# Layer 1 of group 7 as seven block products, with one tail group worked a period earlier, in a fused attention and MLP kernel

## The chip, the cores and the metric

The kernel runs on one core of a Trainium2 chip. The metric is the device time of one execution in microseconds (us). The core's engines run side by side, each with its own queue in program order: PE (TensorE, the matmuls, with its weight loads listed apart as PEld), DVE (VectorE), ACT (ScalarE), POOL (GpSimd) and SP (SyncE, which here only issues transfers). They meet through semaphores. PSUM, the matmuls' output memory, holds 8 banks in this kernel's pools and is full.

## What is computed

Sliding-window attention over 8 batches of 8 heads, 576 positions and 64 channels, and then, over each position's 512 channels, a normalisation and a two-layer MLP with a residual:

```python
scores = q @ k^T / 8                    # per batch and head
mask   = (rel >= 0) & (rel < 64)        # rel = query position - key position
x      = softmax(where(mask, scores, -1e9)) @ v       # heads side by side: 512 channels
xn     = (x - mean) / sqrt(var + 1e-6) * g_ln
out    = x + relu(xn @ w_ch1) @ w_ch2   # w_ch1 is 512 x 2048, w_ch2 2048 x 512
```

## The kernel before, in words

The positions are worked in nine groups of 512. Groups 0 to 7 are the first 512 positions of each batch. Group 8 collects the last 64 positions of all batches; it is built from four "tail groups" of two batches each, numbered 0 to 3. Each group's rows are four blocks of 128 (`kb`).

The loop over `g` (line 950) is called a period here. Period g does the MLP of group g on PE, and threads into it the attention of batch g+1, loads for later batches, and the parts of tail groups. The MLP is a list of `units`; after unit i the functions put into slot i by `at(i, ...)` are issued. So the order on every engine is written out by hand: units and slots say it, and nothing is reordered later. From the trace, periods 5 to 8 begin with PE's first layer-1 matmul at 181.39, 212.20, 240.53 and 266.98 us.

**Attention of a block**: `s_pe` (L319) puts scores into PSUM, `s_exp` (L355) takes the exponential on ACT, `s_mask` (L367) multiplies with the mask on DVE, `b_pe` (L380) multiplies with v on PE, `b_rows` (L402) divides by the sum and takes mean and variance on DVE, `z_step` (L436) normalises on POOL into `z`, and `zt_step` (L471) transposes z into `zT` by a transfer that SP issues. For a batch `part_vB` (L202) also makes a shifted copy of v by two transfers. For a tail group `load_tail` (L97) issues six transfers on SP, `cast_tail` (L111) makes a memset and three casts on POOL, and `t_tail` (L291) transposes, for tail groups 2 and 3 by transfers. `TAILS` (L949) says which tail group is worked in which period: 0 in period 3, 1 in period 5, and 2 and 3 in period 7. In periods 3 and 5 the tail takes part in the branch at line 1116; for period 7 the loop at line 1162 issues both.

**Layer 1** of periods 3 to 7 is `l1` (L501), 16 units: four matmuls of 512 columns into one of two PSUM buffers with the tag "mm", then a relu on ACT into `hrT`. All four blocks of `zT` are read by each matmul.

**Layer 2** is `stage` (L599), seven block products (Strassen's scheme in Winograd's form): the 2x2 blocks of hrT and of w2 are combined by sums on DVE (`s_sums`, L541, and `w2_sums`), and `product(n, p)` (L556) runs eight matmuls of 256 columns, in the order n = 4, 1, 2, 6, 5, 7, 3. The accumulators are pA and pB (tag "mm") and pC (tag "t1"). `post` (L589) and `post_both` (L583) add an accumulator to the residual on DVE, and `store` (L538) sends the rows out.

**Period 8** (group 8) also does layer 1 by seven block products. The sums of w1 are made by `w1_sums` (L805, four tensors of 128x2048 elements), those of zT by `z_sums` (L817). For each of four blocks d of the hidden dimension `l1_product(n, d)` (L675) runs four matmuls of 256 columns. There are three accumulators per d: A takes products 1, 6, 7 and 4 in turn, B product 2, C products 5 and 3. Between them partial sums are taken out. These are the parts:

- `l1_a1(d)`: product 1 to A, copied by ACT to s1; product 2 to B; DVE adds B + s1, POOL takes the relu.
- `l1_a2(d)`: product 5 to C, copied by ACT to s5. `l1_a` is a1 and a2.
- `l1_b(d)`: product 6 onto A, copied by ACT to u2; product 3 onto C; DVE adds C + u2 and takes the relu.
- `l1_c(d)`: product 7 onto A; DVE adds A + s5 and takes the relu.
- `l1_e(d)`: product 4 onto A; ACT takes the relu (L746).

After the first block the order is a(d), c(d-1), b(d), e(d-1). Accumulator A lies in the two "sc" buffers (those of the scores) for d = 0, 1 and 3 and in an "mm" buffer for d = 2; B in "t0"; C in "xps" and "t1" in turn. The plan of period 8 is a generator that is begun at the end of period 7 (`begin_last`, L944). It sets its s_sums and the layer-2 stages in the order 1, 2, 6, 5, 7, 4, 3, the first two parts of product 1 between the last layer-1 products.

Of the kernel before, what the change touches and what calls it, by code (L numbers as in the profile page):

```python
# [18 lines left out]
def kernel(  # L19
# [10 lines left out]
    nc = tc.nc  # L30
# [464 lines left out]
    def mlp_units(g, split=0, three=False, seven=True):  # L495
        hrT = p_hrt.tile([128, NHC, 512], FP16, tag="hrT", name=f"hrT_{g}")
        hv = hrT[:, :, :].rearrange("p (c e) t -> p c e t", e=2)
        sS = {}
        units = []

        def l1(hc):  # L501
            hps = ps_mm.tile([128, 512], FP32, tag="mm", name=f"hps_{g}_{hc}")
# [53 lines left out]
        def product(n, p):  # L556
            which, a, wv = {
                1: ("A", hv[:, :, 0, 0:256], w2v[:, :, 0, 0, :]),
                2: ("B", hv[:, :, 1, 0:256], w2v[:, :, 1, 0, :]),
                6: ("A", sS[2], wT[2]),  # L560
                5: ("C", sS[1], w2v[:, :, 0, 1, :]),
                7: ("A", sS[3], wT[3]),
                4: ("B", hv[:, :, 1, 256:512], wT[4]),
                3: ("C", sS[4], w2v[:, :, 1, 1, :]),
            }[n]
            first = n in (1, 2, 5, 4)
            if p == 0 and n in (1, 2 if last else 4, 5):
                if which == "C" and last:
                    for r in range(2):
                        bank[("C", r)] = ps_t.tile([128, 256], FP32, tag=f"t{r}", name=f"pC{r}_{g}")  # L570
                elif which == "C":
                    bank[which] = ps_t.tile([128, 2, 256], FP32, tag="t1", name=f"p{which}_{g}")
                else:
                    bank[which] = ps_mm.tile([128, 2, 256], FP32, tag="mm", name=f"p{which}_{g}")
            split_c = last and which == "C"
            o = bank[(which, p)][:, :] if split_c else bank[which][:, p, :]
            for c in range(NHC // 2):
                nc.tensor.matmul(  # L578
                    out=o, lhsT=a[:, c, 128 * p:128 * p + 128], rhs=wv[:, c, :],
                    start=(first and (p == 0 or split_c) and c == 0), stop=(c == NHC // 2 - 1), skip_group_check=True,  # L580
                )
# [93 lines left out]
        def l1_product(n, d):  # L675
            w1v = w1g[:, :, :].rearrange("p (a k) (i e m) -> p a k i e m", a=2, e=2, m=128)
            t1, t2, t3, t4 = (zS["sum"][:, m] for m in range(4))
            z = zT[g]
            which, a, b = {
                1: ("A", w1v[:, 0, :, :, 0, :], z[:, 0:2, 0:256]),  # L680
                2: ("B", w1v[:, 1, :, :, 0, :], z[:, 2:4, 0:256]),
                5: ("C", w1S[1], t1),
                6: ("A", w1S[2], t2),
                3: ("C", w1S[4], z[:, 2:4, 256:512]),
                7: ("A", w1S[3], t3),
                4: ("A", w1v[:, 1, :, :, 1, :], t4),
            }[n]
            if n == 1:
                pool, tag = (ps_mm, "mm") if d == 2 else (ps_s, "sc")
                lbank[("A", d)] = pool.tile([128, 2, 256], FP32, tag=tag, name=f"lA_{d}")  # L690
            elif n == 2:
                lbank[("B", d)] = ps_t.tile([128, 2, 256], FP32, tag="t0", name=f"lB_{d}")
            elif n == 5:
                if d % 2:
                    lbank[("C", d)] = ps_t.tile([128, 2, 256], FP32, tag="t1", name=f"lC_{d}")
                else:
                    lbank[("C", d)] = ps_x.tile([128, 4, 256], FP32, tag="xps", name=f"lC_{d}")[:, 0:2]
            o = lbank[(which, d)]
            for r in range(2):
                for kc in range(2):  # L700
                    nc.tensor.matmul(  # L701
                        out=o[:, r, :], lhsT=a[:, kc, 2 * d + r, :], rhs=b[:, kc, :],
                        start=(n in (1, 2, 5) and r == 0 and kc == 0), stop=(kc == 1), skip_group_check=True,
                    )
# [43 lines left out]
        if last:  # L748
# [53 lines left out]

    w1S = {}

    def w1_sums(*which):  # L805
        wv = w1g[:, :, :].rearrange("p (a k) (i e m) -> p a k i e m", a=2, e=2, m=128)
        a11, a12, a21, a22 = (wv[:, b, :, :, a, :] for a, b in ((0, 0), (0, 1), (1, 0), (1, 1)))
        for n in which:
            w1S[n] = p_in.tile([128, NKC // 2, NHC // 2, 128], FP16, tag=f"qk32_{n % 2}", name=f"w1S{n}")
            o = w1S[n][:, :, :, :]  # L810
            x, y, op = {1: (a21, a22, ALU.add), 2: (w1S.get(1), a11, ALU.subtract),
                        3: (a11, a21, ALU.subtract), 4: (a12, w1S.get(2), ALU.subtract)}[n]
            nc.vector.tensor_tensor(out=o, in0=x, in1=y, op=op)

    zS = {}

# [129 lines left out]
        rest, _ = mlp_units(NGRP - 1)  # L946

    rest = None
    TAILS = {3: [0], 5: [1], 7: [2, 3]}  # L949
    for g in range(NGRP):  # L950
        if g == NGRP - 1:
            for _ in rest:
# [5 lines left out]
        def at(i, f, *a):  # L958
            slots[min(i, len(slots) - 1)].append((f, a))
# [156 lines left out]
        elif g > 1 and b < B:  # L1116
# [4 lines left out]
            at(2, s_pe, b, 2)  # L1121
            at(2, s_exp, b, 2, 0, 1)
            at(3, s_mask, b, 2)
            if tail:
                r, i = NGRP - 1, tail[0]
# [24 lines left out]
                at(7, z_step, b, 1)  # L1150
            if g + 2 < B:
                at(5, alloc_qkT, g + 2)
                at(5, after_mask, *((NGRP - 1, tail[0]) if tail else (b, 3)))
# [5 lines left out]
                at(i, z_step, b, j)  # L1159
            for j in range(4):  # L1160
                at((2, 14, 18, {3: 25, 5: 25}.get(b, 23))[j], zt_step, b, j)
        for n, i in enumerate(TAILS.get(g, ()) if b >= B else ()):
            ts = (13, 13, 17, 22) if n else (1, 2, 5, 11)
            at(ts[0], s_mm, NGRP - 1, i)
            at(ts[1], s_mask, NGRP - 1, i)
            at(ts[2], b_step, NGRP - 1, i)
            at(ts[2], z_step, NGRP - 1, i)
            at(ts[3], zt_step, NGRP - 1, i)
        n = g + 2
        if g > 1 and n < B:  # L1170
            if g > 2:
# [22 lines left out]
        for n, i in enumerate(TAILS.get(g + 1, ())):  # L1194
            if n == 0:
                at(15 if g == 2 else 4, load_tail, i)
                at(24 if i < 2 else 18, cast_tail, i)
                at(27 if i < 2 else 22, t_tail, i, 0)
                at(29 if i < 2 else 22, t_tail, i, 1)
            else:  # L1200
                at(25, load_tail, i)
        if len(TAILS.get(g, ())) == 2:
            at(3, cast_tail, TAILS[g][1])
            at(7, t_tail, TAILS[g][1], 0)
            at(7, t_tail, TAILS[g][1], 1)
# [44 lines left out]
```

## Time and profile before

| what | us |
|---|---|
| median of 3 runs (299.96 to 300.1) | 300.01 |
| the profiled execution | 300.26 |
| its span, first to last instruction | 298.5 |
| outside the span | 1.76 |
| mean granted TensorE clock | 0.996 |

The profile is of one execution. Its page gives the busy time of each engine, the chain of work that ended last (followed back from the last instruction to what released it) and the costliest groups of instructions. The trace behind it answers with timelines: start, duration, engine, line, operation, output<-input, shape, count, and in brackets the idle time before and what ended it. Starts are counted from the span's start. A PE row's duration is longer than its share of the engine, because matmuls overlap: the share is the distance to the next row's start. Layer 1 of group 7 runs from 240.53 to 256.01 us on PE, layer 2 from there to 270.11 with the first products of group 8 between.

### The profile page before, as it was taken

The page shows a single profiled execution, that of the slowest core. Times are in us where ns is not written, and L with a number is a line of the kernel's source. Part 1 is how long each engine was busy: PE and PEld are TensorE (multiplying, and loading weights), DVE is VectorE, ACT ScalarE, POOL GpSimd, SP SyncE. Part 2 cuts the span into 40 slices and gives each one's busy share as a digit, 9 for nine tenths or more (in the row PEclk, how much of TensorE's full clock was granted, in tenths as well). Part 3 has the DMA queues.
Part 4 walks back from the last instruction along what each step waited for, and adds up shares of the span by engine and source line. Part 5 has one row for each costly group of instructions (what it writes and reads, how often), then busy time and mean ns, then how long its engine had stood idle before and what let it go on. Part 6 is the DMA issues. An engine that isn't in the chain of part 4 may idle for free.

```text
span 298.5 us, 7825 instructions
## 1 busy us (share of the span) xinstructions
PE 290.9 (97%) x3187; PEld 206.8 (69%) x3187; DVE 218.1 (73%) x413; ACT 154.3 (52%) x261; POOL 166.5 (56%) x244
## 2 busy tenths in 40 slices
PE   8989999999999999999999999999999999999994
PEld 3657545788888888557854786469646854788883
DVE  2881358789994794489767865699568785789983
ACT  3566647677449625873276428841674056305500
POOL 4688889763850987289508860897048407024300
PEclk9999999999999999999999999999999999999998
DMA  8999999979979999899299998991729396003014
GB/s 190 261 377 342 367 302 285 237 226 297 196 168 295 250 133 220 278 222 177 49 308 256 194 176 278 279 162 40 221 50 182 71 185 187 20 18 143 1 37 107
DMA packets 113223, 58.11 MB, mean 195 GB/s; under 512 B 82593, under 2 KB 104161, under 8 KB 113186
## 3 DMA queue, kind: packets, MB, share of 16 engines
q1 hardware_dynamic: 112752, 57.21, 79.1%
q8 instruction: 25, 0.41, 0.6%
q10 hardware_dynamic: 434, 0.40, 0.4%
q14 instruction: 12, 0.10, 0.1%
HBM read 38.80 MB, written 9.44 MB: 162 GB/s over the span
## 4 chain that ended last, share of the span: by engine, by line
PE 93%; DVE 4%; POOL 1%; ACT 1%; issue 0%; POOLq 0%
PE hps L504 26%; PE pA L578 14%; PE hph L645 12%; PE pB L578 10%; PE pC L578 9%; PE xps L399 4%; PE sc L352 3%; PE ch L662 3%; PE tp L279 3%; PE lA L701 2%; PE warm L872 2%; PE lC L701 1%; PE ch L516 1%; PE ztp L481 1%; DVE stats L429 1%; DVE xn L423 1%
## 5 line engine op out<-in xcount | busy, mean ns | idle before, releaser
L504 PE MATMUL hps<-zT,w1g 128*128 128x512 f16 x352 | 80.2, 379 | 0.0
L508 ACT ACTIVATE hrT<-hps 128x512 f16<-128x512 f32 x88 | 52.8, 600 | 36.8 <-PE hps L504 33.8
L504 PEld LDWEIGHTS <-w1g 128*128 128x128 f16 x352 | 33.2, 98 | 38.0 <-issue 1.7
L578 PEld LDWEIGHTS <-sS 128*128 128x128 f16 x512 | 49.3, 98 | 5.6
L362 ACT ACTIVATE pt<-sc 128x512 f16<-128x512 f32 x72 | 39.8, 603 | 22.7 <-PE sc L352 22.3
L451 POOL TENSOR_SCALAR rsz<-mvg 128x1 f32<-128x1 f32 x32 | 10.2, 320 | 61.3 <-DVE mvg L432 51.7
L578 PEld LDWEIGHTS <-hrT 128*128 128x128 f16 x384 | 36.7, 98 | 7.0 <-ACT hrT L508 0.8
L372 DVE TENSOR_TENSOR pt<-pt,mask 128x1024 f16<-128x1024 f16 x32 | 23.9, 753 | 19.6 <-ACT pt L362 19.6
L645 PE MATMUL hph<-zT,w1g 128*128 128x256 f16 x320 | 37.9, 273 | 0.0
L157 POOL CAST qk<-qk 128x1024 f16<-128x1024 f32 x29 | 32.4, 1138 | 8.6 <-PE sc L352 6.0
L645 PEld LDWEIGHTS <-w1g 128*128 128x128 f16 x320 | 30.4, 98 | 4.5 <-POOL w1g L233 0.2
L578 PE MATMUL pC<-w2s,sS 128*128 128x256 f16 x256 | 31.2, 273 | 0.0
L578 PE MATMUL pA<-wT,sS 128*128 128x256 f16 x256 | 30.9, 273 | 0.0
L650 ACT ACTIVATE hrT<-hph 128x512 f16<-128x512 f32 x40 | 24.1, 606 | 10.9 <-PE hph L645 10.7
L260 ACT COPY qkT<-tp 128x1024 f16<-128x1024 f16 (+1 forms) x18 | 17.3, 962 | 23.0 <-PE tp L279 21.3
L552 DVE TENSOR_TENSOR sS<-hrT 128x1024 f16<-128x1024 f16 (+2 forms) x41 | 26.8, 654 | 1.8 <-ACT hrT L508 1.7
L423 DVE TENSOR_TENSOR xn<-xps,rcp 128x256 f32<-128x256 f32 (+1 forms) x50 | 25.8, 539 | 1.5 <-DMA out_dram<-xn 0.8
L429 DVE BATCH_NORM_STATS2 stats<-xn 128x6 f32<-128x512 f32 x36 | 25.0, 694 | 1.2
L457 POOL TENSOR_SCALAR z<-xn,rsz 128x512 f16<-128x512 f32 x24 | 22.3, 927 | 2.5
L452 POOL TENSOR_TENSOR rsz<-rsz,mhalf 128x1 f32<-128x1 f32 x32 | 20.9, 652 | 2.7
L185 POOL CAST vA<-v 128x1024 f16<-128x1024 f32 (+1 forms) x18 | 16.9, 957 | 4.5 <-DMA v<-in_v_dram 4.3
L399 PEld LDWEIGHTS <-pt 128*64 128x64 f16 x576 | 11.5, 110 | 9.1 <-issue 4.7
(121 smaller groups left out, 423.9 us busy)
## 6 DMA issues: line engine op xcount, KB each, us to landing
qk<-in_q_dram SPq DMA_DIRECT2D x16, 512.0 KB, 6.1
qk<-in_k_dram SPq DMA_DIRECT2D x16, 512.0 KB, 7.3
out_dram<-xn SPq DMA_DIRECT2D x32, 256.0 KB, 3.8
v<-in_v_dram SPq DMA_DIRECT2D x28, 256.0 KB, 7.5
w2s<-in_moe_w_ch_dram SPq DMA_DIRECT2D x9, 512.0 KB, 8.5
w1s<-in_moe_w_ch_dram SPq DMA_DIRECT2D x4, 512.0 KB, 7.3
tk<-in_k_dram SPq DMA_DIRECT2D x8, 256.0 KB, 4.4
tv<-in_v_dram SPq DMA_DIRECT2D x8, 256.0 KB, 5.1
```

The costliest lines, as they stand in the source:

```text
L157: nc.gpsimd.tensor_copy(out=dst[:, :].rearrange("p (a j) e d -> p a e j d", j=j), in_=t[:, :].rearrange("p (a e j d) -> p a e j d", e=2, j ...
L362: nc.scalar.activation(out=o, in_=i, func=AF.Exp, bias=0.0, scale=scale)
L372: nc.vector.tensor_tensor(out=ptv, in0=ptv, in1=mb, op=ALU.mult)
L399: nc.tensor.matmul(out=tiles[h // n][64 * r:64 * r + 64, h % n, :D + 1], lhsT=pt[:, par, hp, r, :], rhs=rhs, start=True, stop=True)
L423: nc.vector.tensor_tensor(out=xn[:, n * i:n * i + n], in0=xps[:, :, 0:D], in1=rcp_b, op=ALU.mult)
L429: nc.vector.bn_stats(out=stats, in_=xv)
L504: nc.tensor.matmul(out=hps, lhsT=w1g[:, kc, 128 * hc:128 * (hc + 1)], rhs=zT[g][:, kc, :], start=(kc == 0), stop=(kc == NKC - 1),)
L508: nc.scalar.activation(out=hrT[:, hc, :], in_=hps, func=AF.Relu, bias=0.0, scale=1.0)
L552: nc.vector.tensor_tensor(out=o, in0=x, in1=y, op=op)
L578: nc.tensor.matmul(out=o, lhsT=a[:, c, 128 * p:128 * p + 128], rhs=wv[:, c, :], start=(first and (p == 0 or split_c) and c == 0), stop=(c ...
L645: nc.tensor.matmul(out=hps[:, e], lhsT=w1g[:, kc, 128 * hc:128 * (hc + 1)], rhs=zT[g][:, kc, 256 * half:256 * half + 256], start=(kc == 0) ...
L650: nc.scalar.activation(out=hrT[:, 2 * i:2 * i + 2, 256 * half:256 * half + 256], in_=hps, func=AF.Relu, bias=0.0, scale=1.0)
```

## The change

Period 7 (group NGRP-2) and period 8 are now both "mixed". Period 7's units are layer 1 by seven block products and then the stages in the order 1, 2, 6, 5, 7, 4, 3. The sums of w1 are made in periods 5 and 6 instead of 7, zT's sums are now also made for group 7, at the end of period 6. Tail group 2 is worked in period 6, in the same branch as those of periods 3 and 5, and so is loaded, cast and transposed in period 5; tail group 3 stays in period 7 and is loaded, cast and transposed in period 6. In period 7 accumulator A takes "mm" for every d. In period 7 product 4 of layer 2, and with it the stores of rows 2 and 3, come later than before, and the first units of period 8 one slot later.

```diff
+        mixed = g >= NGRP - 2
...
-            if p == 0 and n in (1, 2 if last else 4, 5):
+            if p == 0 and n in (1, 2 if mixed else 4, 5):
...
-                store(2)
-                store(3)
+                if not mixed:
+                    store(2)
+                    store(3)
...
+                elif mixed:
+                    store(2)
+                    store(3)
...
-                pool, tag = (ps_mm, "mm") if d == 2 else (ps_s, "sc")
+                pool, tag = (ps_mm, "mm") if d == 2 or not last else (ps_s, "sc")
...
+        if mixed:
+            def with_sums(f, a, c0, n):
+                f(*a)
+                s_sums(c0, c0 + 4, n)
+
+            units = [lambda: l1_a1(0), lambda: l1_a2(0), lambda: l1_b(0)]
+            for d in range(1, 4):
+                units += [lambda d=d: l1_a(d), lambda d=d: l1_c(d - 1), lambda d=d: l1_b(d), lambda d=d: l1_e(d - 1)]
+            units[10] = lambda: with_sums(l1_e, (1,), 0, 1)
+            units += [
+                lambda: with_sums(stage, (1, 0), 0, 2), lambda: with_sums(l1_c, (3,), 4, 1),
+                lambda: stage(1, 1), lambda: with_sums(l1_e, (3,), 4, 2),
+                lambda: stage(2, 0), lambda: stage(2, 1),
+            ]
+            for n, m in ((6, 3), (5, 4)):
+                for p in range(2):
+                    units.append(lambda n=n, m=m, p=p: with_sums(stage, (n, p), 4 * p, m))
+            for n in (7, 4, 3):
+                for p in range(2):
+                    units.append(lambda n=n, p=p: stage(n, p))
+            return units, s_sums
...
-    TAILS = {3: [0], 5: [1], 7: [2, 3]}
+    TAILS = {3: 0, 5: 1, 6: 2, 7: 3}
...
-        for n, i in enumerate(TAILS.get(g, ()) if b >= B else ()):
-            ts = (13, 13, 17, 22) if n else (1, 2, 5, 11)
-            at(ts[0], s_mm, NGRP - 1, i)
-            at(ts[1], s_mask, NGRP - 1, i)
-            at(ts[2], b_step, NGRP - 1, i)
-            at(ts[2], z_step, NGRP - 1, i)
-            at(ts[3], zt_step, NGRP - 1, i)
+        if g == NGRP - 2:
+            r, i = NGRP - 1, TAILS[g]
+            at(0, s_pe, r, i)
+            at(2, s_exp, r, i, 0)
+            at(3, s_exp, r, i, 1)
+            at(4, s_mask, r, i)
+            at(7, b_pe, r, i, "sc")
+            at(7, b_rows, r, i)
+            at(7, z_step, r, i)
+            at(11, zt_step, r, i)
...
-        if g > 2:
+        if 2 < g < NGRP - 2:
...
+        if g + 1 in TAILS:
+            i = TAILS[g + 1]
+            at(15 if g == 2 else 4, load_tail, i)
+            at((24, 24, 14, 18)[i], cast_tail, i)
+            at((27, 27, 20, 22)[i], t_tail, i, 0)
+            at((29, 29, 20, 22)[i], t_tail, i, 1)
+        if g == NGRP - 4:
+            at(23, w1_sums, 3, (0,))
+            at(25, w1_sums, 3, (1,))
+        if g == NGRP - 3:
+            at(0, w1_sums, 1)
+            at(3, w1_sums, 2)
+            at(25, w1_sums, 4)
+            at(28, z_sums, NGRP - 2, 1, 2)
+            at(29, z_sums, NGRP - 2, 3, 4)
         if g == NGRP - 2:
-            at(0, w1_sums, 1, 2)
-            at(3, w1_sums, 3)
-            at(21, w1_sums, 4)
-            at(27, z_sums, NGRP - 1, 1, 2)
-            at(28, z_sums, NGRP - 1, 3, 4)
-            at(27, begin_last)
-            at(28, lambda: next(rest))
+            at(25, z_sums, NGRP - 1, 1, 2)
+            at(27, z_sums, NGRP - 1, 3, 4)
+            at(28, begin_last)
+            at(29, lambda: next(rest))
```

In the units of the change a(d) is unit 3, 7 and 11 for d = 1, 2 and 3, and the others follow in the order above: c(d-1), b(d), e(d-1).

More of the change, by code (lines that the diff above doesn't have):

```diff
@@ L688, in l1_product @@
             if n == 1:
-                pool, tag = (ps_mm, "mm") if d == 2 else (ps_s, "sc")
-                lbank[("A", d)] = pool.tile([128, 2, 256], FP32, tag=tag, name=f"lA_{d}")
+                pool, tag = (ps_mm, "mm") if d == 2 or not last else (ps_s, "sc")
+                lbank[("A", d)] = pool.tile([128, 2, 256], FP32, tag=tag, name=f"lA_{g}_{d}")
             elif n == 2:
-                lbank[("B", d)] = ps_t.tile([128, 2, 256], FP32, tag="t0", name=f"lB_{d}")
+                lbank[("B", d)] = ps_t.tile([128, 2, 256], FP32, tag="t0", name=f"lB_{g}_{d}")
             elif n == 5:
                 if d % 2:
-                    lbank[("C", d)] = ps_t.tile([128, 2, 256], FP32, tag="t1", name=f"lC_{d}")
+                    lbank[("C", d)] = ps_t.tile([128, 2, 256], FP32, tag="t1", name=f"lC_{g}_{d}")
                 else:
-                    lbank[("C", d)] = ps_x.tile([128, 4, 256], FP32, tag="xps", name=f"lC_{d}")[:, 0:2]
+                    lbank[("C", d)] = ps_x.tile([128, 4, 256], FP32, tag="xps", name=f"lC_{g}_{d}")[:, 0:2]
             o = lbank[(which, d)]
@@ L803, with w1_sums @@
     w1S = {}
-    def w1_sums(*which):
+    def w1_sums(n, ks=(0, 1)):
         wv = w1g[:, :, :].rearrange("p (a k) (i e m) -> p a k i e m", a=2, e=2, m=128)
         a11, a12, a21, a22 = (wv[:, b, :, :, a, :] for a, b in ((0, 0), (0, 1), (1, 0), (1, 1)))
-        for n in which:
+        if n not in w1S:
             w1S[n] = p_in.tile([128, NKC // 2, NHC // 2, 128], FP16, tag=f"qk32_{n % 2}", name=f"w1S{n}")
[L810 to L813, printed above, removed]
+        x, y, op = {1: (a21, a22, ALU.add), 2: (w1S.get(1), a11, ALU.subtract),
+                    3: (a11, a21, ALU.subtract), 4: (a12, w1S.get(2), ALU.subtract)}[n]
+        k = slice(ks[0], ks[-1] + 1)
+        nc.vector.tensor_tensor(out=w1S[n][:, k], in0=x[:, k], in1=y[:, k], op=op)
     zS = {}
@@ L1123 @@
             at(3, s_mask, b, 2)
-            if tail:
-                r, i = NGRP - 1, tail[0]
+            if tail is not None:
+                r, i = NGRP - 1, tail
                 at(2, s_pe, r, i, False, "t")
@@ L1152 @@
                 at(5, alloc_qkT, g + 2)
-                at(5, after_mask, *((NGRP - 1, tail[0]) if tail else (b, 3)))
+                at(5, after_mask, *((NGRP - 1, tail) if tail is not None else (b, 3)))
                 at(5, cast_qk, g + 2, 0)
@@ L1193 @@
                 at((15, 15, 20, 22)[i - 1], s_sums, 6, 8, i)
[L1194 to L1205, printed above, removed]
-        if g == NGRP - 2:
-            at(0, w1_sums, 1, 2)
-            at(3, w1_sums, 3)
-            at(21, w1_sums, 4)
-            at(27, z_sums, NGRP - 1, 1, 2)
-            at(28, z_sums, NGRP - 1, 3, 4)
-            at(27, begin_last)
-            at(28, lambda: next(rest))
+        if g + 1 in TAILS:
[13 more added lines that the diff above has]
+            at(29, z_sums, NGRP - 2, 3, 4)
+        if g == NGRP - 2:
+            at(25, z_sums, NGRP - 1, 1, 2)
+            at(27, z_sums, NGRP - 1, 3, 4)
+            at(28, begin_last)
+            at(29, lambda: next(rest))
         for i, u in enumerate(units):
```

## The prediction

> **What bounds the kernel now.** I read the page first (busy time, then the chain that ended last), then TensorE's timeline over the last three periods, and the other engines' timelines beside it.
>
> ```profile
> PE 290.9 (97%) x3187; PEld 206.8 (69%) x3187; DVE 218.1 (73%) x413; ACT 154.3 (52%) x261; POOL 166.5 (56%) x244
> ...
> PE 93%; DVE 4%; POOL 1%; ACT 1%; issue 0%; POOLq 0%
> ```
>
> PE is busy for 97% of the span and makes 93% of the chain. So a matmul removed is worth its full time, and a wait added in front of one costs its full time. The stage of the change, from the table of stages (period 7, then period 8 to the end):
>
> ```profile
> 240.70:267.14 26.44, 26.44 (x226) 16.58 (x225) 19.13 (x32) 11.30 (x20) 7.89 (x12) 1.00 0.51 110
> 267.14:298.50 31.36, 26.89 (x241) 23.04 (x238) 23.97 (x44) 9.21 (x16) 6.05 (x4) 0.96 0.23 68
> ```
>
> Columns: span, then busy us of PE, PEld, DVE, ACT, POOL, granted clock, DMA. Period 7 has no hole on PE: 26.44 of 26.44 us. Period 8 already does layer 1 by seven products, the form that period 7 is to get, so it prices the new work. Its rows on PE, ACT and the weight loads:
>
> ```profile
> 246.78 7.08 PE L504 MATMUL hps<-zT,w1g 128*128 128x512 f16 x32
> ...
> 272.30 1.04 PE L701 MATMUL lA<-zsums,w1S 128*128 128x256 f16 x8
> 273.17 0.60 PE L701 MATMUL lC<-zT,w1S 128*128 128x256 f16 x4
> ...
> 282.78 0.60 PE L701 MATMUL lA<-zsums,w1g 128*128 128x256 f16 x4
> ```
> ```profile
> 283.41 0.60 ACT L746 ACTIVATE hrT<-lA 128x512 f16<-128x512 f32 x1 [2.14 <-PE lA L701]
> ```
> ```profile
> 284.06 0.99 PEld L578 LDWEIGHTS <-hrT 128*128 128x128 f16 x10 [0.31 <-ACT hrT L746]
> ```
>
> The reader is to see two prices. A 512-column matmul takes 7.01/32 = 0.219 us (to the next row's start, 253.79), a 256-column one 0.109 (8 in 0.87 us, 272.30 to 273.17). And what PE pays when it must wait for the relu behind product 4: four matmuls issued from 282.78 leave PE's issue free at 283.22, ACT starts at 283.41, ends at 284.01, PE goes on at 284.06. That is **0.84 us** from the end of issue.
>
> **Part 1, fewer columns.** Period 7's layer 1 was 64 matmuls of 512 columns. On PE's timeline they take 1.83 + 3.70 + 7.01 + 1.88 = 14.42 us (64 x 0.219 = 14.0, the rest is restarts after scores and attention). It becomes 7 x 4 x 4 = 112 matmuls of 256 columns, 112 x 0.109 = 12.24, and I leave 0.2 for the two interruptions that stay. Term: **-2.0**. Weight loads are no limit: 0.098 us each beside 0.109.
>
> **Part 2, the accumulator banks.** In period 8 the four A accumulators live in three buffers (d 0, 1, 3 in the two "sc", d 2 in "mm"). In period 7 all four take the two "mm" buffers, because the scores of the tail group need "sc". The order of units is a(d), c(d-1), b(d), e(d-1): product 4 of block d-1 (in e) comes right before product 1 of block d+1, which takes the same buffer. So lA of block 2 waits for the relu of block 0, block 3 for that of block 1, the first layer-2 product pA for that of block 2 and pB for that of block 3; the built program has each of these four matmuls wait on ACT at exactly these relus. Nothing of PE stands between, PE runs in order, and everything behind queues. 4 x 0.84 = **+3.4**. Bounds: 4 x 0.6 (the relu alone) = 2.4, and 4 x 1.0 = 4.0 if a copy of ACT stands in front.
>
> **Part 3, product 3 of block 0.** It reuses bank C after ACT's copy (0.59) of product 5. In period 8 half a pC product (0.87 us) lies between; in period 7 only product 6 (0.44). Copy starts 0.63 after product 5's start and ends at 1.22, product 3 would be due at 0.87: **+0.4** (0 to 0.5).
>
> **Part 4, VectorE's queue.** Product 4 of block d-1 adds onto the A bank that VectorE must have read (the sum after product 7). In period 8 that sum is just in time (276.08 to 276.76, PE due at 276.76). In period 7 the rows of the last tail group are put in slot 7, in front of the sum of block 1. The like rows of before:
>
> ```profile
> 258.63 0.20 DVE L419 RECIPROCAL rcp<-xps 128x8 f32<-128x8 f32 x1
> 258.87 0.69 DVE L423 TENSOR_TENSOR xn<-xps,rcp 128x512 f32<-128x512 f32 x1
> 259.59 0.69 DVE L429 BATCH_NORM_STATS2 stats<-xn 128x6 f32<-128x512 f32 x1
> 260.32 0.18 DVE L432 BATCH_NORM_AGGREGATE mvg<-stats 128x2 f32<-128x6 f32 x1
> ```
>
> They are 1.8 us in a queue without gaps. Counting from the period's start with parts 2 and 3 in: attention of the tail ends on PE at 8.6, its rows are done at 10.5, the sum of block 1 at 11.2, and product 4 was due at 9.8. **+1.4** (0.5 if VectorE is ahead by the slack of part 2's waits, 2.2 if the mask of the same tail also runs late). The other new work of period 7 finds room: 12 copies and 4 relus on ACT replace 16 relus (0.60 each); POOL's four relus (1.5 each) end before layer 2 reads them.
>
> **Part 5, one tail group earlier.** On PE it is moved: 0.34 (scores) + 0.38 (attention) leave period 7 and enter period 6. Net 0. But its loads, casts and transposes move into period 5, where POOL and SP are full:
>
> ```profile
> 199.64 1.21 POOL L157 CAST qk<-qk 128x1024 f16<-128x1024 f32 x1
> ...
> 203.47 2.02 POOL L185 CAST vA<-v 128x1024 f16<-128x1024 f32 x2
> ...
> 207.26 0.76 POOL L457 TENSOR_SCALAR z<-xn,rsz 128x512 f16<-128x512 f32 x1
> ```
> ```profile
> 199.59 9.65 SPq L477 DMA_TRANSPOSE zT<-z  x4
> ```
>
> POOL has no gap from 190.05 to 208.02, where z of group 6's last block ends. The tail's memset and three casts go in before the vA casts: 175.87 to 178.51 in period 4 (2.64), 229.44 to 232.60 in period 6 (3.16). So that z ends at 210.7 to 211.2. SP gets 5.0 more us of loads (221.06 to 226.11 in period 6) and two more transposes (1.2 each) ahead of its transpose and is free at about 210.6, no earlier limit. From issue to landing zT takes 2.3 us there; with the tail's transposes in flight 3.2 is also seen. Landed: 213.0 to 214.4. Period 6's first matmul needs all four blocks and was due at 212.1. **+1.3** (0.9 to 2.3; 0 if POOL's z of 2.17 us at 195.25, otherwise 0.76, is short this time and the casts are cheap). vB, issued behind it, lands at 215.5 before the attention that needs it at 216.1.
>
> **Part 6, sums.** The w1 sums (1.22, 1.22, 1.22, 1.47) and four z sums (2.1) go to periods 5 and 6. VectorE idles 1.7 and 2.0 us early in period 6, so the first two are hidden. Late in it the tail's 2.7 us and the 1.47 make VectorE as tight as in period 5, where the post of product 6 ended 0.4 before PE needed it (207.6, 208.03); period 6 has two transposes (0.9) less on PE. **+0.1** (0 to 1). Period 8 starts with z sums earlier: **-0.1**, the wait of 0.18 that it has now.
>
> **Sum**: -2.0 + 3.4 + 0.4 + 1.4 + 1.3 + 0.1 - 0.1 = **+4.5**. The profiled execution took 300.26 (298.5 in the span), so 304.8; it lies 0.25 above the median of the runs, 300.01. Against the median: **304.5**.
>
> **Rivals.** (a) *Part 5 is hidden*, POOL or the landing has slack that I don't see: +3.2, **303.2**; for it speaks that the one z of 2.17 us is 1.4 above its like. Chance 0.25. (b) *VectorE becomes the bound* in both periods 6 and 7: parts 4 and 6 at their upper ends, and landing at its upper end, +4.5 + 0.8 + 0.9 = **306.2**. VectorE would be some 28 us busy of 29 in period 6 (20.2 + 2.7 tail + 3.9 + 0.9 sums). Chance 0.12. (c) *Faster*: the bank waits cost almost nothing, because the relu of one block overlaps matmuls that PE can still run. Then -2.0 and small waits of 0.5, as in period 8 (its 28 products and two halves of pA and of pC take 16.24 us instead of 15.7): **298.5**. It decides where the release costs under 0.4 us instead of 0.84, together with no wait in part 5; the row at 284.06 and the written order speak against it. Chance 0.04. (d) *Same*: the waits just eat the gain, 300 +- 0.6; it needs parts 4 and 5 both at nothing and part 2 at half. Chance 0.03. (e) *The clock drops*: period 7's layer 1 has 5 us of holes in 20, each of 0.4 to 1.4 us. If the gate counted that as idle and halved the clock, 12 us of matmuls would take 24: **316**. The granted clock is 1.00 from 10 to 20 us, where PE is busy 8.68 of 10, with single holes up to 0.85, so I give 0.02. [...] No run here shows such a drop between matmuls.
>
> **How the numbers follow.** The forecast holds 0.54, the rivals 0.25, 0.12, 0.04, 0.03, 0.02. The range, **302.4 to 306.4**, takes in (a), most of (b) and the bounds of parts 2, 4 and 5, and leaves out (c), (d), (e) and the extremes. Faster than before by over 0.2% (0.6 us, about what a measurement can tell from no change): 0.04; within: 0.03; slower: 0.93.
>
> **What the profile after would show.** 112 more L701 matmuls at 0.109 in period 7 and 64 fewer hps. PE holes of about 0.84, released by ACT's relu, before lA of blocks 2 and 3, pA and pB; one of over 1 us released by VectorE's sum of block 1; one of 1 to 2 us before the first hps of period 6, released by the zT transpose. If the four ACT holes are absent, part 2 is wrong and with it the sign. If PE's hole at period 6's start is absent, (a) holds.

## The result and the profile after

| | before | after |
|---|---|---|
| median of the runs, us | 300.06 (6 runs, 299.83 to 300.26) | 310.2 (6 runs, 308.25 to 312.66) |
| the profiled execution, us | 300.26 | 309.08 |
| its span, us | 298.5 | 307.4 |

The ratio is 1.0348, with a 95% interval of 1.0314 to 1.0381. The kernel became slower by 10.1 us; 4.5 had been forecast, with a range up to 306.4. The runs after also spread over 4.4 us, those before over 0.4.

The page of the changed kernel, busy times, the granted clock in 40 slices of 7.7 us, and the chain:

```profile
PE 291.8 (95%) x3235; PEld 212.0 (69%) x3235; DVE 227.3 (74%) x436; ACT 154.2 (50%) x261; POOL 171.1 (56%) x248
...
PEclk9999999999999999999999999999799999999998
```

PE has 48 matmuls more (112 of 256 columns for 64 of 512) and 0.9 us more of busy time in a span 8.9 us longer. So 8.0 of it are holes. One slice, the 29th (215 to 223 us), has a lower clock. The table of stages (periods 6, 7, and 8 to the end):

```profile
216.09:246.92 30.83, 30.83 (x305) 19.63 (x305) 23.08 (x48) 12.38 (x22) 15.79 (x24) 0.94 0.58 127
246.92:275.94 29.02, 24.81 (x243) 20.76 (x241) 24.02 (x48) 10.21 (x18) 7.88 (x8) 1.00 0.12 42
```

Period 7 took 26.45 us before with PE busy throughout; now it takes 29.02 with PE busy for 24.81, that is 4.21 us of holes. Period 6 took 28.33 before and takes 30.83, busy throughout, at a mean clock of 0.94. It also begins later, at 216.09 instead of 212.20. PE's timeline there, and the holes in period 7:

```profile
210.59 1.92 PE L579 MATMUL pC<-w2s,sS 128*128 128x256 f16 x16
216.09 4.45 PE L505 MATMUL hps<-zT,w1g 128*128 128x512 f16 x12 [3.58 <-DMA zT<-z]
```
```profile
253.97 0.60 PE L706 MATMUL lA<-zT,w1g 128*128 128x256 f16 x4 [0.73 <-ACT hrT L751]
...
258.42 0.60 PE L706 MATMUL lA<-zsums,w1g 128*128 128x256 f16 x4 [1.18 <-DVE hrT L721]
259.70 0.60 PE L706 MATMUL lA<-zT,w1g 128*128 128x256 f16 x4 [0.68 <-ACT hrT L751]
...
263.67 1.03 PE L579 MATMUL pA<-w2s,hrT 128*128 128x256 f16 x8 [0.69 <-ACT hrT L751]
...
267.21 1.91 PE L579 MATMUL pB<-w2s,hrT 128*128 128x256 f16 x16 [0.69 <-ACT hrT L751]
```

The bracket is the idle time before a row and what ended it. The last five rows are the forecast's four bank waits and its wait for VectorE. The first fence holds what was not forecast: a hole of 3.58 us where 1 to 2 had been, and behind it twelve matmuls that take 4.45 us where they took 2.78. The windows there (after the busy times come the granted clock and the DMA share):

```profile
217.00:220.00 3.00, 3.00 (x8) 1.06 (x7) 0.00 (x0) 1.19 (x2) 0.00 (x0) 0.50 0.97 308
220.00:222.00 2.00, 2.00 (x53) 1.17 (x52) 0.97 (x3) 1.30 (x3) 0.00 (x0) 0.94 0.55 208
```

Half the clock, from 216.83 to 220.24 us. And SP's timeline ahead of the hole (the issue of transfers, "x2" for two of them):

```profile
194.74 1.50 SPq L106 DMA_DIRECT2D tq<-in_q_dram  x2
196.28 3.63 SPq L109 DMA_DIRECT2D tk<-in_k_dram  x2
199.95 2.29 SPq L109 DMA_DIRECT2D tv<-in_v_dram  x2
202.34 3.76 SPq L268 DMA_TRANSPOSE qkT<-qk  x2
206.20 4.69 SPq L477 DMA_TRANSPOSE zT<-z  x3
211.06 1.19 SPq L297 DMA_TRANSPOSE tqT<-tq  x1
212.35 1.25 SPq L304 DMA_TRANSPOSE tkT<-tk  x1
213.69 1.23 SPq L477 DMA_TRANSPOSE zT<-z  x1
```

The first three rows and the two for tqT and tkT are the tail group's, new in this period. SP is hardly ever free here (one pause of 0.4 us, at 204.4, lies inside the row of qkT), and the last zT is issued at 213.69 although POOL had its z ready at 211.94. POOL is late too, by 3.9 us against the 208.02 of before: the tail's memset and casts stand in front of the casts of vA, and one of them waits for its load.

```profile
203.61 0.17 POOL L118 MEMSET vt<- 128x16 f16 x1
...
205.83 1.04 POOL L121 CAST vt<-tv 128x1024 f16<-128x1024 f32 x1 [0.57 <-DMA tv<-in_v_dram]
206.81 2.67 POOL L185 CAST vA<-v 128x1024 f16<-128x1024 f32 x2
...
211.18 0.76 POOL L457 TENSOR_SCALAR z<-xn,rsz 128x512 f16<-128x512 f32 x1
```

### The profile page after: what moved, and what is told of

Its sections match the earlier page's. It is cut to its first block, busy times and chain, and to the rows that moved or that the text cites. A ratio compares the mean times of both kernels' runs of the same rounds, so it can differ in the third digit from the quotient of the medians.

```text
span 307.4 us, 7978 instructions
## 1 busy us (share of the span) xinstructions
PE 291.8 (95%) x3235; PEld 212.0 (69%) x3235; DVE 227.3 (74%) x436; ACT 154.2 (50%) x261; POOL 171.1 (56%) x248
## 4 chain that ended last, share of the span: by engine, by line
PE 80%; POOL 7%; DMA 3%; SPq 2%; DVE 2%; issue 2%; ACT 2%; POOLq 0%; ACTq 0%
PE hps L505 18%; PE pA L579 12%; PE hph L650 12%; PE pB L579 8%; PE pC L579 8%; PE lA L706 4%; PE sc L352 3%; PE xps L399 3%; PE ch L667 3%; PE tp L279 2%; PE lC L706 2%; DMA qk<-in_k_dram 2%; POOL qk L157 2%; POOL z L457 2%; PE lB L706 1%
## 5 line engine op out<-in xcount | busy, mean ns | idle before, releaser
L505 PE MATMUL hps<-zT,w1g 128*128 128x512 f16 x288 | 67.4, 386 | 3.6 <-DMA zT<-z 3.6
L509 ACT ACTIVATE hrT<-hps 128x512 f16<-128x512 f32 x72 | 43.2, 600 | 25.3 <-PE hps L505 18.6
L505 PEld LDWEIGHTS <-w1g 128*128 128x128 f16 x288 | 27.4, 99 | 35.7 <-DMA zT<-z 3.9
L372 DVE TENSOR_TENSOR pt<-pt,mask 128x1024 f16<-128x1024 f16 x32 | 25.3, 799 | 14.6 <-ACT pt L362 14.6
L650 PEld LDWEIGHTS <-w1g 128*128 128x128 f16 x320 | 30.4, 98 | 4.6 <-POOL w1g L233 0.3
L723 POOL TENSOR_SCALAR hrT<-hrT 128x512 f16<-128x512 f16 x8 | 11.9, 1487 | 31.9 <-DVE hrT L721 29.3
L553 DVE TENSOR_TENSOR sS<-hrT 128x1024 f16<-128x1024 f16 (+2 forms) x39 | 25.9, 664 | 0.3 <-ACT hrT L509 0.3
L457 POOL TENSOR_SCALAR z<-xn,rsz 128x512 f16<-128x512 f32 x24 | 23.0, 959 | 2.5
L419 DVE RECIPROCAL rcp<-xps 128x4 f32<-128x4 f32 (+1 forms) x51 | 7.9, 178 | 18.0 <-PE xps L399 17.9
```

The source lines that it names most:

```text
L372: nc.vector.tensor_tensor(out=ptv, in0=ptv, in1=mb, op=ALU.mult)
L457: nc.gpsimd.tensor_scalar(out=z, in0=xv, scalar1=rs, scalar2=nm, op0=ALU.mult, op1=ALU.add)
L505: nc.tensor.matmul(out=hps, lhsT=w1g[:, kc, 128 * hc:128 * (hc + 1)], rhs=zT[g][:, kc, :], start=(kc == 0), stop=(kc == NKC - 1),)
L509: nc.scalar.activation(out=hrT[:, hc, :], in_=hps, func=AF.Relu, bias=0.0, scale=1.0)
L650: nc.tensor.matmul(out=hps[:, e], lhsT=w1g[:, kc, 128 * hc:128 * (hc + 1)], rhs=zT[g][:, kc, 256 * half:256 * half + 256], start=(kc == 0) ...
```

## The experiments

Two theories stood at the start. **A**: the miss belongs to the moved tail group: SP's queue makes the hole, and the hole costs the clock. **B**: it belongs to layer 1 by seven products and its sums (VectorE late in two periods). "Period 6's start" below is PE's first layer-1 matmul of that period, 212.20 before and 216.09 after.

**1. The tail's move alone.** Layer 1 of group 7 as before, the sums as before:

```diff
-        mixed = g >= NGRP - 2
+        mixed = g >= NGRP - 1
```

> Only the move of tail group 2 is kept; layer 1 of group 7, the sums of w1 and zT and the order of layer 2 are those of before. Theory: the late zT of period 6 (SP's queue, filled with the tail's loads and transposes) and the half clock behind the hole cost about 5.4 us whatever layer 1 of group 7 does. Expected 305.5 us, PE's hole at the start of period 6 at 3.5 us and the first hps of period 6 at a granted clock of 0.5. Rival: the hole comes from the new sums and layer 1, or from both together, and the tail alone is the +1.3 of the prediction: 301.4 us.

Measured 304.4 us (ratio 1.0153, 1.0121 to 1.0184), nearer to the theory's 305.5 than to the rival's 301.4. PE at the start of period 6:

```profile
215.15 4.36 PE L505 MATMUL hps<-zT,w1g 128*128 128x512 f16 x12 [3.18 <-DMA zT<-z]
```

POOL's z ends at 210.66 here, as forecast, but the last zT is issued at 212.70, behind the tail's transposes. So the hole and the clock belong to the tail's move, and the other 5.8 us of the change come with layer 1 and its sums.

**2. The tail's transposes behind the last zT.**

```diff
-            at((27, 27, 20, 22)[i], t_tail, i, 0)
-            at((29, 29, 20, 22)[i], t_tail, i, 1)
+            at((27, 27, 25, 22)[i], t_tail, i, 0)
+            at((29, 29, 25, 22)[i], t_tail, i, 1)
```

> The changed kernel, with the two transposes of tail group 2 issued in slot 25 of period 5 instead of 20, so that SP issues them behind the last zT of group 6. Theory (SP's queue is the bound): the zT is issued at 212.0, where POOL's z ends, lands at 214.3, the hole shrinks from 3.6 to about 2.0 us, and a hole that short leaves the clock at 1.00: 306.8 us. Rival (POOL's z is the bound, SP only follows): the zT is issued no earlier, no change, 310.2. Second rival (the first matmuls are slow for another reason than the hole's length): 1.7 gained, not 3.4, 308.5.

Measured 310.1 us (1.0307, against the same runs of before). PE's timeline of this kernel:

```profile
214.46 2.78 PE L505 MATMUL hps<-zT,w1g 128*128 128x512 f16 x12 [2.09 <-DMA zT<-z]
219.46 0.23 PE L399 MATMUL xps<-vB,pt 128*64 128x65 f16 x1 [2.22 <-DMA vB<-vA]
...
220.04 0.61 PE L352 MATMUL sc<-qkT,qkT 64*128 64x64 f16 x16
...
221.01 1.46 PE L505 MATMUL hps<-zT,w1g 128*128 128x512 f16 x3
```

The last zT is issued at 212.02, right behind POOL's z (212.00), the hole shrinks to 2.09 us, and the twelve matmuls behind it run at the full clock. So the theory's first step holds, and it divides the hole of 3.58 us: 2.09 stay with POOL's late z, 1.5 were SP's queue. The time is still that of the rival, for another reason. The transfers that build vB now stand behind the tail's transposes (SP issues them at 215.92), the attention of batch 7 waits 2.22 us for them, and behind this second hole the clock is halved after all (0.50 from 219.24 to 222.65). Layer 1 goes on at 221.01, only 0.4 us earlier than without the edit, and its next three matmuls take 1.46 us. What stood last in SP's queue paid: zT with the hole of 3.58 us in the change, vB with one of 2.22 here.

**3. The hole filled with matmuls on zeros** (16 of 512 columns at the end of period 5; they write a bank that nothing reads):

> The changed kernel, with 16 dummy matmuls of 512 columns (3.5 us, on constants, into a fresh buffer that nothing reads) at the end of period 5, in PE's hole. Theory (the idle hole makes the clock gate halve the clock): the hole's length stays, but the matmuls after it run at 0.219 us and a granted clock of 1.00: 1.7 us faster than the change, 308.5. Rival (the first hps are slow because transfers crowd their reads, or for another reason): they stay at 0.43 us each, 310.2 or slower.

Measured 308.25 us (1.0274). In this kernel's timeline the same late start is followed by a full clock:

```profile
212.29 3.62 PE L1258 MATMUL hole<-wfill 128*128 128x512 f16 x16
215.74 2.79 PE L505 MATMUL hps<-zT,w1g 128*128 128x512 f16 x12
```

So it was the idle time that took the clock there: the twelve matmuls take 2.79 us behind the filled hole and 4.45 behind the idle one, 1.7 us more. But this execution shows the clock fall elsewhere, in period 7 behind the holes of 1.18 and 0.69 us (PE's rows, then windows of 3.41 us with the granted clock third from the end):

```profile
254.70 0.60 PE L706 MATMUL lC<-zT,w1S 128*128 128x256 f16 x4
256.48 0.60 PE L706 MATMUL lA<-zsums,w1g 128*128 128x256 f16 x4 [1.18 <-DVE hrT L721]
257.77 0.91 PE L706 MATMUL lA<-zT,w1g 128*128 128x256 f16 x4 [0.69 <-ACT hrT L751]
...
258.48 1.06 PE L706 MATMUL lB<-zT,w1g 128*128 128x256 f16 x4
```
```profile
254.49:257.90 3.41, 1.54 (x14) 1.08 (x12) 3.27 (x9) 1.19 (x2) 2.78 (x5) 1.00 0.01 2
257.90:261.31 3.41, 3.41 (x18) 2.35 (x17) 1.52 (x3) 1.17 (x2) 1.16 (x2) 0.50 0.24 43
261.31:264.70 3.39, 2.71 (x25) 2.28 (x24) 2.54 (x5) 1.18 (x2) 0.60 (x1) 1.00 0.00 0
```

Rows that take 0.60 us elsewhere take 0.91 and 1.06, and period 7 takes 30.6 us instead of 29.0.

**4. Period 7's holes filled too**, with two matmuls on zeros in each of the slots 6, 10, 14 and 18, beside those of experiment 3:

> The changed kernel with dummy matmuls of 512 columns on constants in PE's holes: 16 at the end of period 5, and 2 each before lA of blocks 2 and 3, before pA and after product 4 of block 3 (0.44 us each place, within waits of 0.7), into buffers that nothing reads. The waits themselves stay. Theory (the clock gate counts the holes): the granted clock stays 1.00 in periods 6 and 7 in every execution, all matmuls run at full rate, 306.9 us, and the runs lie within 0.5 us of each other instead of 4. Rival (the clock in period 7 falls for the load itself, whatever PE does in the holes): 308.3 as with the first hole alone filled.

Measured 307.43 us (1.0249, 1.0233 to 1.0266), all runs within 1.25 us. Mean clock 0.998 in the profiled execution (0.992 after), 0.997 to 1.0 in the four runs, and period 7 takes 29.0. So the clock stays up with the holes filled, as the theory says; the time lies between its 306.9 and the rival's 308.3, and the spread is more than its 0.5. Do such drops also explain the 4.4 us of spread of the changed kernel, and its median, 1.1 above the profiled execution, which had no drop in period 7? In part. The mean clock is on record for every run: 0.992 and 0.993 in its two fastest runs and 0.986 to 0.988 in the four others, which fits one more drop in those. But two runs with 0.987 and 0.988 took 309.6 and 312.66 us, and in experiment 3 the slowest run, 310.17, had 0.997. The rest of the spread has another cause, which stays open.

**5. The order of a block's products** in period 7: 2, 5, 1, so that two products stand between product 4's relu and the next user of its bank; likewise the last layer-1 products ahead of pA and pB. It was timed in one execution.

```diff
-                units += [lambda d=d: l1_a(d), ...
+                units += [lambda d=d: l1_251(d), ...
...
-                lambda: with_sums(stage, (1, 0), 0, 2), lambda: with_sums(l1_c, (3,), 4, 1),
-                lambda: stage(1, 1), lambda: with_sums(l1_e, (3,), 4, 2),
+                lambda: with_sums(l1_c, (3,), 4, 1), lambda: with_sums(stage, (1, 0), 0, 2),
+                lambda: with_sums(l1_e, (3,), 4, 2), lambda: stage(1, 1),
```

> The changed kernel, with period 7's block order 2, 5, 1 in place of 1, 2, 5 for d = 1 to 3, and product 7 of block 3 put before the first half of layer 2's product 1, product 4 of block 3 before the second half: two products (0.87 us) now lie between each relu's product 4 and the matmul that takes its bank for blocks 2 and 3 and pB, one (0.44) for pA. Theory: three of the four waits of 0.7 vanish and the fourth is 0.3; period 7, from its first layer-1 matmul to that of group 8, takes 26.6 instead of 29.0 us. Rival (the wait is in fact that of VectorE's sums, the bank only comes last): the holes move to the products behind and the period stays within 0.6 of 29.0.

It took 309.12 us (the profiled execution after took 309.08), and period 7 29.3, which is the rival's figure. The bank waits are gone but for 0.25 at pA, and the wait for VectorE in front of product 4 of block 1 grew from 1.18 to 2.08, with half the clock behind it (0.50 from 260.29 to 263.70):

```profile
259.05 0.60 PE L706 MATMUL lA<-zsums,w1g 128*128 128x256 f16 x4 [2.08 <-DVE hrT L721]
```

One wait had hidden part of another. The rival's figure is in part luck: the drop costs 1.7 us (half of 3.41), and without it the period would be 27.6, an estimate, midway between theory and rival.

**6. The same, and the tail's rows behind layer 1** (slot 18 instead of 7):

> The changed kernel with the block order of the earlier order run, and with the tail's rows on VectorE moved from slot 7 to slot 18 of period 7 (behind layer 1), its scores from slot 0 to slot 1, zT's sums for group 8 to slots 27 and 28. Period 6's late start stays. Theory: the hole before product 4 of block 1 (1.18, or 2.08 in the order run) goes, the bank waits too, so period 7 takes 26.5 us instead of 29.0, PE is never idle long enough in it to lose the clock, and the time is 306.3 us (310.2, less 2.5 for the waits, less 1.4 for the clock in most executions). Rival (VectorE is full in layer 1 whatever the order): holes of 1 us or more move to the next sums, and the period stays above 28.

Measured 306.1 us (1.0216, 1.0187 to 1.0245); period 7 takes 26.49, as expected. With both kinds of wait taken away period 7 still only equals the 26.45 of before, with one tail group less in it.

**7. and 8. The tail groups in periods 3, 4, 5 and 7**, so that period 6 has none; number 8 has the edits of experiment 6 as well:

```diff
-    TAILS = {3: 0, 5: 1, 6: 2, 7: 3}
+    TAILS = {3: 0, 4: 1, 5: 2, 7: 3}
```

> The changed kernel with the tail groups 0 to 3 worked in periods 3, 4, 5 and 7 instead of 3, 5, 6 and 7, and tail 2 transposed on PE as 0 and 1 are (0.7 us of PE). Nothing of a tail is loaded, cast or transposed in period 5, so period 6 starts as before. Theory: the 5.4 us of period 6's start go, layer 1 by seven products as written stays a loss: 300.1 + 2.5 (waits less columns) + 0.7 (transposes) + 1.4 (half clock in period 7 in most executions) = 304.7 us. Rival (layer 1 by seven products is a gain once period 6 starts in time): below 300.

> Both: the tail groups in periods 3, 4, 5 and 7, and the block order and the rows' place of the run before. Theory: no hole at period 6, period 7 at 26.0 to 26.5 us with one tail in it, no clock loss: 300.1 - 2.0 (columns) + 0.5 (left-over waits) + 0.7 (transposes on PE) - 0.1 = 299.2 us. Rival (every earlier period loses as much by its new tail as period 6 did): 302 or more.

Measured 309.84 (1.0328) and 306.55 us (1.0208). Both missed; for number 8 the rival's time (302 or more) came. Period 6 takes 28.33 us again, but in number 7 period 4 takes 35.0 instead of 30.8 and period 3 32.3 instead of 30.7 (33.8 and 33.0 in number 8). PE and POOL of number 7 in period 4:

```profile
181.68 0.40 PE L481 MATMUL ztp<-ident,z 128*128 128x128 f16 x4 [2.18 <-POOL z L457]
```
```profile
180.85 0.77 POOL L457 TENSOR_SCALAR z<-xn,rsz 128x512 f16<-128x512 f32 x1 [2.27 <-DMA zT<-z]
```

There are three z buffers, and each is free only when the transfer that transposes it has read it. SP issues these transfers behind the tail's loads; so POOL waits for them (2.27 us in the row above), and PE for POOL (2.18). In each of the three periods in which it was tried (3 and 4 here, 5 in the change), fetching one tail group while working another beside a batch to load cost time. (Before, periods 3 and 5 worked one and periods 2, 4 and 6 fetched.)

**9. Tail group 2 out of period 5**: loaded behind everything else there, cast and transposed in period 6, its rows late in period 6.

> The changed kernel with tail group 2 taken out of period 5: its loads are issued behind everything else of period 5, its casts and transposes come in slots 9 and 10 of period 6, its scores in slot 17 and its rows in slot 23; tail group 3 is loaded and cast a little later in period 6. Layer 1 of period 7 is left as in the change. Theory (the hole at the start of period 6 and the half clock behind it come from the tail's loads and transposes that stand on SP's queue ahead of the last zT): period 6 starts again at 212.2 instead of 216.1, its first twelve matmuls take 2.7 instead of 4.45 us, period 7 stays at 29.0 to 30.6: 310.2 less 5.4 is 304.8. Rival (period 6 has no room for casts, transposes and rows of one tail and the loads of the other; VectorE becomes late behind its seven-product sums): period 6 takes 31 to 32 us instead of 29, and the time is 306.5 to 308.

**10. The same with the edits of experiment 6.**

> The kernel before this one and, in period 7, the two mends that together brought it to 26.5 us (per block the products in the order 2, 5, 1; the tail's rows behind layer 1). Theory (the two losses are separate and add): 306.1 less the 5.4 of period 6's start, 300.7. With both losses gone layer 1 by seven products is worth almost nothing: period 7 takes 26.5 us as it did before the change. Rival (period 6 is too full with a whole tail in it): 302 to 303.5.

**11. The same with four A banks** instead, in the order of the change, and the tail's attention behind layer 1:

```diff
-                pool, tag = (ps_mm, "mm") if d == 2 or not last else (ps_s, "sc")
+                pool, tag = (ps_mm, "mm") if (d == 2 if last else d < 2) else (ps_s, "sc")
```

> Tail group 2 out of period 5 as in the two kernels ahead, the products of a block in the order of the change (1, 2, 5), but the four A accumulators of period 7 in four banks (two mm, then two sc), and the last tail's attention put into slot 20, behind the layer-1 products that need the sc banks. Theory (what is left of period 7's holes, 1.7 us in seven holes of 0.25 to 0.34, is waits on a bank or on the copy of product 1 that stands too close; with four banks and the order 1, 2, 5 they go, and the 2 us of columns come out as time): period 7 takes 24.9 to 25.3 us and the time is 299.2, below the 300.0 before the change. Rival (VectorE is busy for 23 of these 25 us and sets the pace, and the late tail delays the sums of zT that period 8 starts with): period 7 and the start of period 8 give it back, 300.5 to 301.5.

Measured 307.73 (1.0223), 305.5 (1.0178, 1.0153 to 1.0203) and 302.99 us (1.0106, 1.007 to 1.0142). In all three, period 6 starts at 211.8 to 212.6 with the twelve matmuls in 2.78 us, so that part of theory A held. But period 6 takes 31.75 us, which in number 9 is the rival. Numbers 10 and 11 missed both of their figures; in number 10 period 7 takes 27.99 instead of 26.5, with new waits of 0.77 and 0.41 us near its start. The rows of number 11:

```profile
230.95 0.41 PE L352 MATMUL sc<-tqT,tkT 64*128 64x64 f16 x16 [1.12 <-DMA tkT<-tk]
...
237.06 0.45 PE L399 MATMUL xps<-vt,pt 128*64 128x65 f16 x16 [1.23 <-DVE pt L372]
...
246.50 0.60 PE L706 MATMUL lC<-zsums,w1S 128*128 128x256 f16 x4 [1.55 <-DVE zsums L857]
247.77 0.60 PE L706 MATMUL lC<-zT,w1S 128*128 128x256 f16 x4 [0.20 <-ACT zsums L718]
```

My placement made four new waits, 4.1 us together. Behind the last of them period 7 has no hole listed at all: with four banks the order of the change runs through.

**12. Number 11 with these four waits mended** (scores and rows of tail group 2 two slots later, one w1 sum earlier, zT of group 7's last block ahead of the last tail's transposes on SP):

> The kernel with four A banks and tail group 2 out of period 5, its remaining holes mended: in period 6 the scores of tail group 2 two slots later (1.12 us of waiting for its transposes), its attention two slots and its rows two slots later and the last w1 sum earlier (1.23 us of waiting for the mask on VectorE); and zT of group 7's last block on SP ahead of tail group 3's transposes and between its loads, with that tail's scores in slot 2 of period 7 (1.55 and 0.20 us at the start of period 7). The computation is the same. Theory (each of these four holes is a wait that the order made, so they go and nothing takes their place): 302.99 less 4.1 is 298.9, period 7 takes 24.8 to 25.2 us, and the change's columns come out as time, 0.3 per cent below the kernel before. Rival (period 6 has VectorE busy nearly throughout, so that rows and sums put later come late for the last products or for the first of period 7): half comes back, 300.5 to 301.5, above the kernel before.

Measured 300.56 us (1.001, 0.9996 to 1.0024): the rival's time, and no difference from before. Its table of stages for periods 6 and 7, and PE in period 7:

```profile
212.29:241.91 29.62, 29.50 (x307) 19.13 (x305) 26.88 (x52) 12.66 (x23) 16.46 (x26) 1.00 0.78 168
241.91:267.65 25.74, 24.56 (x242) 20.60 (x240) 23.29 (x46) 9.89 (x18) 10.22 (x11) 1.00 0.24 57
```
```profile
244.05 0.60 PE L708 MATMUL lC<-zT,w1S 128*128 128x256 f16 x4 [0.23 <-ACT zsums L720]
245.02 0.41 PE L354 MATMUL sc<-tqT,tkT 64*128 64x64 f16 x16 [0.37 <-DMA tkT<-tk]
...
251.84 0.60 PE L708 MATMUL lA<-zsums,w1g 128*128 128x256 f16 x4 [0.54 <-DVE hrT L723]
```

Period 7 gains 0.71 on the 26.45 of before, and that is no more than the tail work that left it (scores 0.34, attention 0.39). Period 6 loses 1.29 on its 28.33: 0.73 is that same work, and the other 0.56 is not traced to rows. So nearly all of the change's 10 us were waits that an order made and an order takes away. What is left is an exchange: 1.9 us of columns for as much in small waits and restarts, of which the three holes above are 1.14. What the change would be worth without these three was not tried. No version tried was faster than before.

## Why the prediction was wrong

The direction was right, and the sum failed at one term and one rival. Waits are measured from row to row, less 0.435 us for a group of four matmuls.

- **Part 1, columns** (-2.0): period 7 grew by 2.57 us while 0.72 of tail work left it and waits of 5.17 (below) came. That leaves -1.88, by subtraction; against period 7 of experiment 1 (25.54, with the same tail work) it leaves -1.7. Right.
- **Part 2, four bank waits** (+3.4): 252.64 to 253.97, 258.42 to 259.70, 262.39 to 263.67 and 265.93 to 267.21 are 1.33, 1.28, 1.28 and 1.28, less 0.435 each: 3.43. Right. The row that gave the price was read too simply: at 283.21 PE went on with pB (16 matmuls in 1.96 us until the next row, usually 1.75), and it was a weight load that stood until 284.06. As the time from the end of issue to the first dependent work 0.84 holds, and in period 7 there was nothing to put in between.
- **Part 3** (+0.4): 0.40. **Part 4, VectorE** (+1.4): 256.64 to 258.42 less 0.435 is 1.35. Right. Experiment 5 adds what the sum could not show: part 4's wait starts behind part 2's, so taking away the one feeds the other.
- **Part 5, the tail group a period earlier** (+1.3, bounds 0 to 2.3): this is the step that failed. It measured 5.4, beyond its upper bound: 3.7 by the later start of period 6 (period 5 takes 34.55 instead of 30.81) and 1.7 by the clock. The prediction put POOL's z at the end of the chain and said of SP that it "is free at about 210.6, no earlier limit". z came at 211.94, 0.7 to 1.2 later than forecast, and by experiment 2 this alone leaves a hole of 2.09, still inside the bounds. SP was the limit: it came free at 213.65, 1.7 behind z, so that the hole became 3.58 and cost the clock. SP was 3.0 late, for the most part by this: I had priced the six loads at 5.0 us from period 6, where the same rows ran with a DMA share of 0.82; in period 5 they took 7.5 at a share of 0.97 (the two tk issues 3.63 instead of 1.25). The transposes of qk, 3.9 instead of 5.1, gave 1.2 of that back, and the three zT transposes behind them took 4.9 instead of 3.6. I had the tail's transposes in the queue, but not what it means that SP has almost no gap from 193.5 on: past POOL's z, what SP is late goes to zT, here 1.7 us.
- **Part 6** (sums, 0.1 and -0.1): the rest of period 6 grew by 0.84, that is 0.72 of tail work and 0.12; period 8 took 25.06 instead of 25.17. Right. Rival (b), VectorE as the bound, did not occur.
- **Rival (e), the clock**, had a chance of 0.02 and the price of a whole layer at half the clock, 12 us (316 in all). It came in small: 1.7 us behind the long hole in period 6, and 1.6 in period 7 in some of the executions. I took a stretch with single holes up to 0.85 us as the evidence; it said nothing on holes of 1.2 and 0.7 close together, nor on one of 3.6.

So 4.5 forecast, plus 2.4 for the later start and 1.7 for the clock behind it, is 8.6 of the 8.8 us of the profiled execution. The median lies another 1.1 higher. A drop in period 7, as experiments 2, 3 and 5 show it, costs 1.6 and fits the mean clock of four of the six runs; it does not explain how far these four lie apart.

## What to carry to other kernels

Price a moved step on the queue that it is moved into, not on the one that it came from: SP's queue, almost without gaps, came free 1.7 us behind POOL's z, and zT's hole was 3.58 us instead of 2.09; and the same six loads took 7.5 us to issue at a DMA share of 0.97 instead of 5.05 at 0.82 (that the share is the reason is not shown). Two queues can end close together, as POOL (211.94) and SP (213.65) did here: price both, and not only the later one. On an engine that is busy for 97% of the time, ask of every new hole how much idle time it makes, with its neighbours, within 3.41 us, the length of the drops here: 2.16 us in one hole (experiment 2) and 2.19 in two (experiment 3) cost the clock as well, 1.6 us more in period 7 of experiment 3. And a scheme that saves multiplications by cutting a long accumulation into short dependent ones must be given enough banks: here 3.4 us of bank waits stood against 2.0 of columns.

## What the runs showed of the hardware

- In the drops between matmuls the granted clock went to 0.50 and stayed there for 3.41 us: 216.83 to 220.24 in the changed kernel, 215.00 to 218.41 in experiment 1, 219.24 to 222.65 in experiment 2, 257.90 to 261.31 in experiment 3, 260.29 to 263.70 in experiment 5. In the changed kernel it fell to 0.50 again at 305.57, behind the last matmul: 85.33 us after it had come back, which is 25 times 3.413. Experiment 2 has a second drop, from 260.20; its two drops begin 40.96 us apart, 12 times 3.413. This fits changes of the clock on a grid of 3.41 us, and drops that begin at 216.83 and 215.00 would put the grid at another place in each execution. That is an inference from these times.
- PE's idle time in the 3.41 us ahead of a drop, with 0.109 us for a matmul of 256 columns and 0.219 for one of 512, was 2.68 us in the changed kernel, 3.21 in experiment 1, 2.16 and 2.19 in experiment 2, 2.19 in experiment 3 and 2.17 in experiment 5. So PE was not idle throughout in any of them. In experiment 3 it was 1.34 and 0.85, together 2.19, from 254.49 to 257.90, and the clock fell. In the changed kernel the same holes lie differently: from 257.79 to 261.20 (12 steps of 3.413 behind the drop's start) it was 0.63 and 0.84, together 1.47, and the clock stayed. In experiment 2 the hole of 2.09 us gave 2.04 from 212.42 to 215.83, and the clock stayed; the hole of 2.22 gave 2.16 in the next stretch, to 219.24, and it fell. So holes of the same size cost the clock in one execution and not in another. That their place on a grid decides it is my reading of these traces; no experiment moved a hole to test it.
- With two matmuls on zeros in each of four holes of period 7 the clock was 1.00 there in experiment 4, and they cost no time (period 7 took 29.01 us, 29.02 after). In experiment 3, without them, it fell to 0.50 in period 7 of the profiled execution, which then took 30.6 us, 1.6 more.
- SP's issue of the six loads of a tail group took 5.05 us at a mean DMA share of 0.82 and 7.5 at 0.97, the two tk loads among them 1.25 and 3.63. That the share is the reason is not shown; no run changed it alone.
